# Fixed orders of instructions up to the end of a kernel with LSH attention and two expert layers

## The chip, the core and the metric

The kernel runs on one core of a Trainium2 chip. The metric is the time of one execution on the device in microseconds. Five instruction streams run side by side on the core: TensorE (PE in the profile, its weight loads PEld), VectorE (DVE), ScalarE (ACT), GpSimd (POOL) and SyncE (SP), which here only issues DMAs. Each stream runs in the order in which its instructions were written, and waits for others by semaphores.

## What is computed

The attention works on 2 x 8 heads with 768 positions of width 64. A query sees only the keys of its own hash bucket. The result, 1536 tokens of width 512, goes through two layers without any norm or residual:

```python
x = np.ascontiguousarray(attn_out.transpose(0, 2, 1, 3)).reshape(B * S, H * D)
h = x @ w_in            # 512 -> 2048
x = (h - np.tanh(h)) @ w_out
g = x @ w_gate          # 512 -> 1536
val = x @ w_val
out = (g / (1 + np.exp(-g)) * val) @ w_out2
```

## The kernel before

All work is declared as operations: each call of `op` in the kernel notes the engines that may do it with an assumed time for each, what it reads and writes, and a due time. An operation is one instruction or a short run of them, and in what follows it is named by its number in the order of declaration, 0 to 3380. Operations 0 to 1342 are the attention, 1343 to 3380 the two layers. `Plan.order` (line 182) then plays the operations through once while the program is built, and the sequence that comes out is written into the five instruction streams. Nothing of it is decided at run time.

`ORDER` (line 66) holds a written list of operations for each engine. As long as an engine's list lasts, the engine takes its next listed operation and no other. After that it takes, among the operations that are ready by the assumed times, the one with the earliest due time, and one that two engines may do goes to the one that is free:

```python
                if at[e] < len(ORDER[e]):
                    n = ORDER[e][at[e]]
                    if n not in can or e in ops[n][8] and port > now + 1e-9:
                        continue
                    at[e] += 1
                else:
                    q = ready.get(e, [])
```

In the kernel before, the lists reach a little beyond the attention: 365 of TensorE's 817 operations, 418 of VectorE's, 350 of ScalarE's, 221 of GpSimd's and 164 of SyncE's 240.

The layers work on two halves of the tokens. A product of an input layer (`products`, line 923) multiplies a 256 x 256 block of weights by a block of the tokens with seven products instead of eight (sums of blocks are formed first, on the weights by `sub`, lines 405 and 407, on the tokens by lines 461 to 468). Each is a group of six matmuls, since every factor is split in a high and a low part (line 955). Its result goes from PSUM to SBUF (ScalarE, lines 884, 891 and 935), is added to another's (VectorE, line 938), goes through tanh or the gate (lines 872 and 877), and is the factor of an output group (`out_group`, line 987, line 1009), again six matmuls: 384 columns wide in the first layer, 512 in the second. Output groups are copied to a staging buffer (line 1038) and added up by an accumulating DMA on GpSimd's queue: line 1046 into SBUF in the first layer, line 1055 into the output in DRAM in the second. Only the last output groups are added by VectorE (lines 1022 and 1033) and stored on SyncE's queue (line 1034).

The weights come as int64 bit patterns of doubles. `convert` (line 358) loads a chunk of 512 KB on SyncE's queue (line 371) into one of two buffers `raw`, and three VectorE instructions make f32 of it (lines 373, 376 and 379). A load waits until the conversion before the last has freed its buffer. The planner assumes 3.5 us to its landing. Splitting in high and low is a copy on ScalarE (lines 385 and 422) and a subtraction on GpSimd or VectorE (lines 387 and 424).

The operations that the prediction names: the additions 1648 and 2360 (line 872) and 2449, 2724, 2935 and 3101 (line 938), which products at the waits read; the loads 2835, 3001, 3073, 3149 and 3315 (line 371) and the first conversion step of three of them, 3002, 3150 and 3316 (line 373); conversion step 2508 (line 376); the accumulating writes 2704, 2810, 2870, 2899, 3036 and 3065 (line 1055); and 2915 (line 405), 3013 (line 387) and 3058 (line 872) ahead of them. A place is the position in TensorE's sequence, counted from 0.

Of the kernel before, what the change touches and what calls it, by code (L numbers as in the profile page):

```python
# [46 lines left out]
def chunk_keys():  # L47
# [5 lines left out]
    for i in range(NP2):  # L53
# [29 lines left out]
    """,  # L83
    DVE="""
# [18 lines left out]
    """,  # L103
    ACT="""
# [15 lines left out]
    """,  # L120
    POOL="""
# [9 lines left out]
    """,  # L131
    SP="""
# [7 lines left out]
    """,  # L140
).items()}

# [1056 lines left out]
```

## Time and profile before

| | |
|---|---|
| time, median of 3 runs | 777.51 us (776.3 to 778.58) |
| the profiled execution | 777.4 us |
| its span, first to last instruction | 775.6 us |
| PE busy | 755.5 us, 97% of the span, 4332 matmuls |
| DVE, ACT, POOL busy | 606.0, 475.6, 332.9 us |
| granted TensorE clock | 1.0 of 2.4 GHz |
| first operation of the layers to start on PE | 233 us |
| start of the product at place 353 | 256.6 us |

A row of a timeline has the start in us from the begin of the span, the length, engine and line of the source, the operation, what it writes and reads by the program's names, shapes, and how many instructions in a row it merges; in square brackets stands the idle time of the engine before it and what ended it. The ends of matmuls are modelled, so that the shown end of a group lies beyond the start of the next.

### The profile page before, as it was taken

The numbers are of one execution on the slowest core, as the hardware profiler recorded it, in microseconds if no ns is written. First come the engines' busy times: TensorE is split into PE (matmuls) and PEld (weight loads), VectorE is DVE, ScalarE is ACT, GpSimd is POOL, SyncE is SP. The second block draws the span as 40 slices with busy tenths as digits, with TensorE's granted clock in tenths as the row PEclk, the third lists the DMA queues.
The fourth block names the chain that finished last, engine by engine and source line by source line (L and its number), as shares of the span: only waits on it lengthen the run. The fifth ranks groups of instructions, "written<-read, shape, count | busy, mean of one in ns | idle before, by whom it ended". The sixth has DMA issues, their size and how long they took to land.

```text
span 775.6 us, 12370 instructions
## 1 busy us (share of the span) xinstructions
PE 755.5 (97%) x4332; PEld 663.4 (86%) x4332; DVE 606.0 (78%) x1092; ACT 475.6 (61%) x975; POOL 332.9 (43%) x357
## 2 busy tenths in 40 slices
PE   5899999999999999999999999999999999999998
PEld 2667676767668999999999999989998998989996
DVE  4988788868897967888778699898887867777355
ACT  3887778888776755565566556655554554555430
POOL 2755676767965712323333224543333332322120
PEclk9999999999999999999999999999999999999999
DMA  5573655356232052878676762333536756754685
GB/s 150 133 194 87 169 153 131 99 129 167 71 135 82 28 136 59 199 180 198 146 183 164 159 154 65 89 106 123 190 85 168 165 110 139 163 110 67 123 169 197
DMA packets 38717, 104.23 MB, mean 134 GB/s; under 512 B 4704, under 2 KB 10080, under 8 KB 38656
## 3 DMA queue, kind: packets, MB, share of 16 engines
q1 hardware_dynamic: 28288, 71.06, 29.7%
q0 software_dynamic: 9904, 31.59, 23.7%
q10 hardware_dynamic: 464, 0.80, 0.5%
q8 instruction: 34, 0.56, 0.3%
q14 instruction: 27, 0.22, 0.1%
HBM read 49.17 MB, written 18.87 MB: 88 GB/s over the span
## 4 chain that ended last, share of the span: by engine, by line
PE 88%; DVE 5%; DMA 3%; ACT 1%; issue 1%; POOL 1%; SPq 0%; ACTq 0%; DVEq 0%; POOLq 0%
PE bs L955 30%; PE t L1009 15%; PE s L746 8%; PE t L776 8%; PE x L799 8%; PE h L1009 8%; PE x L1009 5%; DMA raw<-in_w 2%; PE x L955 2%; PE t L955 2%; DVE m L756 1%; PE h L955 1%; DMA raw<-in_kT 1%; DVE ct L872 1%; PE h L709 1%
## 5 line engine op out<-in xcount | busy, mean ns | idle before, releaser
L955 PE MATMUL bs<-x,wi 128*128 128x384 f32 x1200 | 233.4, 336 | 3.6 <-DVE ct L938 3.6
L955 PEld LDWEIGHTS bs<-x,wi 128*128 128x128 f32 x1200 | 210.4, 188 | 10.8 <-DVE ct L938 5.7
L765 POOL TENSOR_SCALAR ct<-ct,r 128x768 f32<-128x768 f32 x96 | 93.5, 979 | 40.7 <-DVE r L764 28.5
L756 DVE TENSOR_REDUCE m<-s 128x1 f32<-128x768 f32 x96 | 91.1, 952 | 23.0 <-PE s L746 20.5
L746 PE MATMUL s<-op 128*128 128x384 f32 x384 | 93.9, 369 | 1.7 <-ACT ct L758 1.5
L758 ACT ACTIVATE ct<-s,m 128x768 f32<-128x768 f32 x96 | 86.7, 904 | 14.0 <-DVE m L756 7.4
L935 ACT ACTIVATE ct<-bs 128x384 f32<-128x384 f32 x120 | 58.8, 491 | 48.7 <-PE bs L955 48.2
L776 PE MATMUL t<-csb,ct 128*128 128x128 f32 x576 | 82.8, 276 | 1.5 <-DVE pt L782 0.9
L776 PEld LDWEIGHTS t<-csb,ct 128*128 128x128 f32 x576 | 66.7, 140 | 20.3 <-POOL ct L765 6.0
L746 PEld LDWEIGHTS s<-op 128*128 128x128 f32 x384 | 65.3, 193 | 16.1 <-ACT ct L758 9.8
L1009 PE MATMUL t<-op,wo 128*128 128x384 f32 x384 | 76.5, 335 | 0.0
L782 ACT ACTIVATE pt<-t 128x384 f32<-128x384 f32 x129 | 60.3, 492 | 26.2 <-PE t L776 25.9
L799 PE MATMUL x<-pt,v 128*64 128x384 f32 x384 | 69.0, 495 | 0.0
L1009 PEld LDWEIGHTS t<-op,wo 128*128 128x128 f32 x384 | 67.2, 188 | 0.8 <-DVE op L872 0.4
L1009 PE MATMUL t<-wo,op 128*128 128x512 f32 x264 | 67.8, 393 | 0.0
L387 POOL TENSOR_TENSOR wi<-fs,wi 128x512 fp32r<-128x512 f32 (+1 forms) x27 | 42.1, 1559 | 57.0 <-ACT wi L385 57.0
L872 POOL TENSOR_TENSOR ct<-ct 128x384 f32<-128x384 f32 x22 | 23.0, 1046 | 82.7 <-ACT ct L891 62.7
L1009 PEld LDWEIGHTS t<-wo,op 128*128 128x128 f32 x264 | 48.9, 188 | 7.9
L1046 POOL DMA_DIRECT2D acc<-ct x24 | 21.0, 875 | 72.3 <-ACT ct L1038 29.4
L385 ACT ACTIVATE wi<-fs 128x512 fp32r<-128x512 f32 (+1 forms) x60 | 41.8, 701 | 14.3 <-PE bs L955 4.0
L799 PEld LDWEIGHTS x<-pt,v 128*64 128x64 f32 x384 | 24.7, 136 | 28.7 <-issue 28.5
L955 PE MATMUL bs<-op,wi 128*128 128x384 f32 x240 | 47.5, 335 | 0.0
(165 smaller groups left out, 1385.0 us busy)
## 6 DMA issues: line engine op xcount, KB each, us to landing
raw<-in_w SPq DMA_DIRECT2D x68, 512.0 KB, 3.7
acc<-ct POOLq DMA_DIRECT2D x24, 768.0 KB, 6.0
out<-acc POOLq DMA_DIRECT2D x16, 768.0 KB, 7.6
op<-raw SPq DMA_DIRECT2D x42, 192.0 KB, 3.4
op<-f SPq DMA_DIRECT2D x56, 96.0 KB, 2.6
v<-in_v SPq DMA_DIRECT2D x8, 384.0 KB, 4.1
out<-acc SPq DMA_DIRECT2D x4, 768.0 KB, 3.8
acc<-out SPq DMA_DIRECT2D x4, 768.0 KB, 4.5
```

The source lines that it names most:

```text
L385: op({"ACT": act(n)}, lambda e: e.activation(out=hi, in_=src, func=ACTF.Copy), r=rk, w=[wk + (0,)], due=due, late=late)
L387: op({"POOL": pool(n), "DVE": dve(n)}, lambda e: e.tensor_tensor(out=lo, in0=src, in1=hi.bitcast(F32), op=ALU.subtract), r=rk + [wk + (0,) ...
L746: g.matmul(out=s[:, kh, 0:TB], lhsT=(b, a)[first][:, q0], rhs=ks[kh][0 if first else 1], start=first, stop=not first,)
L756: op({"DVE": 0.87}, lambda g: g.tensor_reduce(out=m, in_=sv, axis=AX.XY, op=ALU.max, negate=True), r=[sk + (0,), sk + (1,)], w=[mk])
L758: op({"ACT": 0.9}, lambda g: g.activation(out=p.rearrange("p (a b) -> p a b", a=2), in_=sv, func=ACTF.Exp, bias=m, accum_out=sm), r=[sk + ...
L765: op({"POOL": 0.91}, lambda g: g.tensor_scalar(out=p, in0=p, scalar1=r, scalar2=1.0, op0=ALU.mult, op1=ALU.mult), r=[pk, rk], w=[pk])
L776: g.transpose(out=t_t[z][:, kt * 128:(kt + 1) * 128], in_=p[:, z * TB + kt * 128:z * TB + (kt + 1) * 128], identity=ident)
L782: g.activation(out=dst, in_=src, func=ACTF.Copy) if g is nc.scalar else g.tensor_copy(dst, src),
L799: g.matmul(out=x[r, :], lhsT=v[:, kt, r], rhs=pt_t[ptks[e][1]][:, kt, :], start=(kt == 0), stop=(kt == NKT - 1), tile_position=(0, 64 * e),)
L935: op({"ACT": act(TB)}, lambda e: e.activation(out=dst, in_=bank(), func=ACTF.Copy), r=[bk], w=dk, due=due)
L955: e.matmul(out=bank(), lhsT=w[:, wpart, wi * 256 + k * 128:wi * 256 + k * 128 + 128], rhs=x_at(sb, xn, xpart, k), start=first and m == 0, ...
L1009: e.matmul(out=ps(), lhsT=lhs, rhs=rhs, start=c == 0, stop=c == 5)
```

## The change

The five written lists go on to the last operation. On TensorE the old list's first 353 entries stay, and then the order is another one up to place 748, and from 749 on as before. 65 operations that VectorE did are in GpSimd's list and 28 of GpSimd's in VectorE's, 25 of ScalarE's are in VectorE's and 13 of VectorE's in ScalarE's. All operations, their shapes, buffers and what they wait for are the same. Of the diff, the lists of GpSimd and SyncE are shown whole, of the others the rows that carry the operations named above:

```diff
--- before.py
+++ after.py
@@ -79,7 +79,29 @@
...
-        1429 1340 1423 1341 1468 1456 1484 1446 1454 1452 1450 1462 1466 1482 1464 1522 1509 1476 1474 1505 1552
+        1429 1340 1423 1341 1468 1456 1484 1446 1454 1462 1450 1482 1452 1466 1464 1522 1474 1509 1476 1489 1511
+        1505 1513 1552 1503 1519 1526 1534 1507 1540 1542 1589 1524 1532 1605 1547 1550 1573 1577 1554 1575 1587
...
+        1656 1711 1696 1704 1671 1698 1675 1694 1709 1727 1725 1707 1719 1754 1741 1737 1717 1732 1745 1743 1735
...
+        2269 2282 2275 2304 2308 2302 2314 2306 2322 2316 2349 2330 2357 2355 2351 2361 2366 2353 2325 2389 2364
+        2387 2395 2368 2401 2391 2399 2405 2407 2397 2414 2417 2412 2437 2441 2448 2439 2453 2457 2479 2473 2477
...
+        2645 2640 2633 2682 2649 2689 2684 2693 2691 2709 2663 2715 2719 2705 2723 2711 2698 2702 2713 2734 2731
...
+        2903 2905 2924 2926 2930 2932 2934 2938 2943 2946 2960 2955 2949 2962 2953 2964 2974 2951 2977 3016 3014
...
+        3090 3063 3096 3100 3104 3071 3109 3112 3115 3117 3119 3121 3126 3128 3130 3135 3140 3143 3147 3161 3180
...
+        3344 3347 3351 3355 3358 3361 3365 3368 3371 3375 3378
...
@@ -98,8 +120,39 @@
...
-        1431 1561 1387 1562 1424 1563 1660 1426 1469 1428 1457 1344 1346 1486 1455 1459 1451 1461 1463 1467 1350
-        1353 1354 1488 1477 1475 1479
+        1431 1561 1387 1562 1424 1563 1660 1426 1469 1428 1457 1463 1344 1455 1459 1451 1461 1486 1565 1467 1483
+        1354 1353 1477 1479 1566 1481 1360 1512 1490 1358 1661 1514 1520 1488 1527 1473 1516 1518 1541 1535 1531
...
+        1789 1648 1697 1672 1801 1790 1712 1791 1802 1714 1699 1803 1701 1710 1703 1805 1729 1720 1906 1806 1907
...
+        2360 2466 2327 2468 2469 2365 2369 2396 2507 2470 2390 2392 2402 2400 2406 2508 2408 2394 2409 2511 2426
+        2416 2418 2413 2422 2509 2442 2449 2443 2411 2445 2454 2458 2456 2450 2427 2452 2430 2512 2460 2429 2513
...
+        2832 2642 2692 2716 2706 2826 2644 2724 2755 2836 2833 2837 2699 2838 2834 2701 2736 2718 2728 2697 2843
...
+        3011 2896 2929 3078 3150 3079 3151 2935 3080 2939 2940 2948 2937 2956 3152 2957 2959 2965 2942 2963 2975
...
+        3160 3031 3169 3170 3033 3029 3048 3060 3175 3068 3240 3241 3062 3242 3050 3093 3177 3244 3040 3316 3095
+        3317 3245 3101 3105 3106 3246 3318 3108 3114 3179 3247 3248 3249 3122 3123 3125 3131 3132 3136 3137 3141
...
+        3379
...
@@ -115,8 +168,33 @@
...
-        1384 1430 1386 1432 1425 1342 1427 1343 1349 1470 1458 1485 1357 1447 1347 1359 1460 1453 1472 1352 1487
-        1483 1465 1523 1510 1355 1567 1478 1506
+        1384 1430 1386 1432 1425 1342 1427 1343 1349 1458 1357 1447 1470 1347 1359 1460 1472 1485 1523 1453 1487
+        1352 1510 1355 1475 1478 1465 1480 1506 1528 1515 1567 1517 1553 1504 1530 1508 1536 1569 1525 1533 1538
...
+        3334 3342 3349
...
@@ -127,7 +205,15 @@
...
-        1445 1315 1400 1333 1335 1325 1496 1404 1502 1422 1406 1433 1564 1345 1471 1351 1348 1358 1360 1356
+        1445 1315 1400 1333 1335 1325 1496 1404 1502 1422 1406 1433 1564 1345 1346 1471 1348 1351 1350 1356 1529
+        1568 1546 1570 1521 1609 1572 1594 1549 1630 1638 1686 1689 1687 1658 1691 1693 1706 1793 1808 1734 1810
+        1716 1812 1753 1761 1781 1910 1916 1829 1931 1839 1932 1857 1876 1884 1904 2033 2039 1952 1960 2054 1962
+        2058 2055 1980 1977 2056 1999 2060 2009 2027 2024 2083 2085 2075 2132 2100 2103 2151 2238 2161 2176 2179
+        2340 2341 2342 2198 2223 2226 2346 2285 2299 2266 2281 2291 2324 2379 2382 2319 2380 2297 2329 2363 2384
+        2321 2420 2386 2421 2434 2404 2472 2424 2518 2520 2493 2590 2591 2592 2594 2539 2567 2662 2673 2674 2679
+        2612 2681 2637 2749 2753 2639 2750 2751 2695 2648 2757 2726 2839 2828 2840 2708 2841 2771 2779 2915 2704
+        2916 2802 2917 2733 2861 2923 2921 2810 2870 3006 2892 2945 3013 2899 2966 3081 3082 3083 2980 3154 2976
+        2968 3087 3171 3172 3173 3058 3036 3111 3065 3103 3142 3251 3202 3326 3224 3231 3269 3277 3298 3303 3343
...
@@ -136,7 +222,11 @@
...
-        1182 1179 1207 1394 1434 1211 1440 1216 1491 1497 1556 1560 1659 1665
+        1182 1179 1207 1394 1434 1211 1440 1216 1491 1497 1556 1560 1659 1665 1677 1782 1681 1788 1800 1804 1905
+        1911 1923 2028 1927 2046 2034 2110 2050 2122 2116 2227 2126 2233 2332 2336 2370 2374 2461 2467 2506 2510
+        2582 2586 2651 2657 2489 2536 2665 2669 2741 2745 2817 2574 2823 2831 2835 2620 2911 2907 2983 2989 2997
+        3001 3073 3077 3149 3155 3163 3167 3239 3243 3315 3321 3328 3352 3362 3330 3338 3372 3346 3354 3357 3360
+        3364 3367 3370 3374 3377 3380
...
```

## Rows read from the trace of the kernel before

**Rows 1.** Chain that ended last: shares on the page, and from 680 us, start, us, what:

```profile
PE 88%; DVE 5%; DMA 3%; ACT 1%; issue 1%; POOL 1%; SPq 0%; ACTq 0%; DVEq 0%; POOLq 0%
...
694.82 1.39 PE t L1009 x6
696.21 3.12 PE bs L955 x18
```

**Rows 2.** TensorE's timeline at the end: start, us, engine line op out<-in xcount:

```profile
768.82 1.52 PE L1009 MATMUL x<-wo,op 128*128 128x512 f32 x6
770.18 1.52 PE L1009 MATMUL h<-wo,op 128*128 128x512 f32 x6
```

**Rows 3.** Windows: stretch, length, busy us of PE, PEld, DVE, ACT, POOL (x), PEclk, DMA, GB/s:

```profile
256.00:776.00 520.00, 511.43 (x2789) 488.82 (x2787) 398.80 (x687) 277.87 (x550) 166.59 (x138) 1.00 0.57 136
500.00:530.00 30.00, 28.27 (x153) 26.59 (x152) 28.52 (x47) 17.20 (x32) 12.33 (x9) 1.00 0.28 90
```

**Rows 4.** TensorE's timeline at its six waits from 256 us on:

```profile
315.78 1.34 PE L1009 MATMUL h<-op,wo 128*128 128x384 f32 x6 [0.30 <-DVE op L872]
...
490.36 1.32 PE L1009 MATMUL h<-op,wo 128*128 128x384 f32 x6 [0.37 <-DVE ct L872]
...
509.02 1.34 PE L955 MATMUL bs<-x,wi 128*128 128x384 f32 x6 [1.73 <-DVE ct L938]
...
586.87 2.37 PE L955 MATMUL bs<-x,wi 128*128 128x384 f32 x12 [0.48 <-DVE ct L938]
...
645.64 1.68 PE L955 MATMUL bs<-x,wi 128*128 128x384 f32 x8 [0.66 <-DVE ct L938]
...
692.47 2.35 PE L955 MATMUL bs<-x,wi 128*128 128x384 f32 x12 [0.71 <-DVE ct L938]
```

**Rows 5.** Waits of TensorE from 256 us on: us in total, times, longest:

```profile
PE bs L955 <- DVE ct L938: 3.6, 4, 1.7
```

**Rows 6.** VectorE's timeline before 692 us:

```profile
690.32 0.43 DVE L373 TENSOR_SCALAR f<-raw 128x512 uint32<-128x512 uint32 x1 [2.33 <-DMA raw<-in_w]
...
691.87 0.55 DVE L938 TENSOR_TENSOR ct<-bs,ct 128x384 f32<-128x384 f32 x1
```

**Rows 7.** Waits of VectorE for weight chunks, from 256 us on:

```profile
DVE fs L373 <- DMA raw<-in_w: 5.8, 4, 3.6
...
DVE f L373 <- DMA raw<-in_w: 5.2, 3, 2.3
```

**Rows 8.** Landing of the loads of line 371 issued at 683.8 us, and at 646.2 us:

```profile
DMA to landing us min/median/max: 6.5/6.5/6.5
...
DMA to landing us min/median/max: 3.4/3.4/3.4
```

**Rows 9.** GpSimd's timeline from 680 us:

```profile
681.36 1.30 POOL L1055 DMA_DIRECT2D out<-acc  x1 [1.23 <-ACT acc L1038]
```

**Rows 10.** DMA issues on the page: issue, xcount, KB each, median us to landing:

```profile
acc<-ct POOLq DMA_DIRECT2D x24, 768.0 KB, 6.0
out<-acc POOLq DMA_DIRECT2D x16, 768.0 KB, 7.6
```

**Rows 11.** VectorE's timeline, three long instructions:

```profile
311.83 2.04 DVE L407 TENSOR_TENSOR fs<-fs 128x256 f32<-128x256 f32 x1
...
502.73 1.79 DVE L373 TENSOR_SCALAR fs<-raw 128x512 uint32<-128x512 uint32 x1
504.44 2.05 DVE L468 TENSOR_TENSOR acc<-acc 128x768 f32<-128x768 f32 x1
```

**Rows 12.** GpSimd's timeline from 310 us:

```profile
311.74 1.84 POOL L387 TENSOR_TENSOR wi<-fs,wi 128x768 fp32r<-128x768 f32 x1
```

**Rows 13.** Source line 407: ns min/median/max, first and last start:

```profile
L407 DVE TENSOR_TENSOR fs<-fs x25: 408/425/2036, 227.2 to 697.5; 128x256 f32<-128x256 f32 x25
```

**Rows 14.** Source line 872, additions on the two engines:

```profile
L872 DVE TENSOR_TENSOR ct<-bs,ct x52: 541/550/558, 248.2 to 759.5; 128x384 f32<-128x384 f32 x52
...
L872 POOL TENSOR_TENSOR ct<-ct x22: 1003/1014/1712, 255.3 to 737.4; 128x384 f32<-128x384 f32 x22
```

61 rows, old and new, of tables (ACT, DVE, PE) are left out of this document.

## The prediction

> **What bounds the kernel now.** I read the page first. The chain that ended last lies on TensorE for 88% of the span, and only small shares are left for the other engines [rows 1]. A busy TensorE is not by itself a TensorE at its peak, so the next view is where nothing disturbs it. In the chain three products of the expert layers (six matmuls of 384 columns each) take 3.12 us, 1.04 us for one, and a group of the second output layer (six of 512 columns) takes 1.39 us [rows 1]; at the end of the program such groups start 1.36 us apart [rows 2]. The shown end of a group lies 0.16 us behind the start of the next (1.52 against 1.36), which has to be added to every idle time of TensorE.
>
> From there the ideal of the stretch that the change can touch can be counted. The new lists differ from what ran before from place 353 of TensorE's list on (places count from 0, operations by their number in order of declaration), which is the product that starts at 256.6 us. From 256 us on there are 2789 matmuls [rows 3]; 72 groups of six are of the 512-column kind, 432 matmuls (six pairs of chunks, two halves of the tokens, six groups each). 2357 x 1.04/6 + 432 x 1.36/6 = 408.5 + 97.9 = 506.4 us, or 508.6 us with 1.39. The stretch runs from 256.0 to the end of the last group, 770.18 + 1.52 = 771.7 us [rows 2], so 515.7 us. **About 7.1 us are lost on TensorE**, and that is nearly all that an order can win here: behind the last product there is one addition and one write, and the lists end in the same order as before.
>
> Where the 7.1 us lie is told by the timeline of TensorE in this stretch: six waits, at 316, 490, 509, 587, 646 and 692 us, all of them for VectorE (DVE below), with 0.30, 0.37, 1.73, 0.48, 0.66 and 0.71 us of idle time [rows 4]. With 0.16 us each they cost 0.46, 0.53, 1.89, 0.64, 0.82 and 0.87 us, in all 5.2 us. Four of the six, 3.6 us of idle time, are for the addition at line 938 [rows 5]. Behind each wait the array also needs a little longer: twelve matmuls from 692.47 on took 2.35 us where 2 x 1.04 + 0.16 = 2.24 are due [rows 4], 0.11 us, and six of these are 0.7 us. That makes 5.9 us; 1.2 us are spread over smaller delays.
>
> **Why DVE is late there** has two causes, and the change has to be weighed against both.
>
> The first is a transfer. The product at 692.47 waits for the addition of operation 3101. On DVE that addition stands behind the first steps of two weight conversions, and the second of these (3316, line 373) had DVE idle for 2.33 us until its weight chunk had landed [rows 6]. In this stretch DVE waits 11.0 us for such landings, 7 times [rows 7]. This load took 6.5 us from issue to landing, another one 3.4 us [rows 8]. The slow one was issued at 683.8, 2.4 us after GpSimd had issued an accumulating write of 768 KB at 681.4, whose landing takes 7.6 us in the median [rows 9, 10]; the fast one had none of these in flight just before. The stalls of TensorE at 587, 646 and 692 us are all of this kind, 2.3 us.
>
> The second cause is crowding on DVE, and instructions of DVE that stand still beside one of GpSimd (locks, below). From 500 to 530 us DVE is busy for 28.5 of 30 us [rows 3]. At 311.83 a block subtraction (line 407) takes 2.04 us where its median is 0.42, beside a GpSimd subtraction that began at 311.74; at 502.73 and 504.44 two DVE instructions take 1.79 and 2.05 us [rows 11 to 13]. The largest stall of TensorE follows at once, the 1.89 us at 509 us. With those at 316 and 490 us the second kind has 2.9 us.
>
> **The change, part by part.** No operation is added or taken away; the lists only fix the order of operations 1343 to 3380 and the engine of those that two engines may do. Nothing is decided at run time, so a longer list costs nothing itself.
>
> Engines. 65 operations go from DVE to GpSimd and 28 come back, 25 go from ScalarE to DVE and 13 back. An addition of 128x384 takes 0.55 us on DVE and 1.01 us on GpSimd [rows 14], so GpSimd gets some 37 x 1.0 = 37 us more on its 166.6 us, 22%, and DVE some 37 x 0.55 - 12 x 0.55 = 14 us less on its 398.8 us [rows 3]. GpSimd's extra time lies beside TensorE: in the new list no product that takes a GpSimd result comes closer than two products behind the sum of GpSimd's work for it. That cover is gone where an addition of GpSimd is followed by a write or a lock.
>
> The loads. The weight loads on SP's queue keep their engine and nearly their order; each still waits for the conversion that frees its buffer. What moves are the accumulating writes on GpSimd's queue. Before, write 2704 can be issued once TensorE has done place 649; now it stands behind 2915, a subtraction that went to GpSimd and whose queue needs place 674. Write 2899 goes from place 699 to 711 (behind 3013), 3036 from 729 to 742 (behind 3058), 3065 from 739 to 749. The three loads that came late, 2835, 3149 and 3315, stay at places 651, 700 and 739. So none of them has a fresh write ahead of it any more; their landing should fall from 6.5 to about 3.4 us [rows 8]. At 690 us DVE would then wait 2.33 - 3.1 < 0, not at all. The additions behind them are late no longer, and next in turn is nothing nearer than the two conversions themselves. This is worth 0.64 + 0.82 + 0.87 + 3 x 0.11 = **2.7 us**. What is late instead are the writes; their staging buffers are taken again 12 products later at the soonest, 12.5 us against 7.6. In the first layer two writes get only 6 products (6.2 us) where 9 were usual, and their landing takes 6.0 us in the median [rows 10]: up to half a microsecond of waiting for the engine that fills the buffer again, with the product that needs it five places off, so nothing on TensorE.
>
> The crowding. Before place 592 (509 us) the old list has 14 DVE operations after the product at place 583, and DVE ran from 500 to 509 us without a pause; the new one has 14 operations for products from place 581 on, two products (2.1 us) more room, and conversion step 2508 stands earlier. The operations ahead of places 409 and 576 are pulled apart in the same way (1648 is now needed at place 413 and not 409). All three gone is worth 0.46 + 0.53 + 1.89 + 3 x 0.11 = **3.2 us**. Of the 1.2 us of small delays I take 0.5 as gone, since those behind 587 us follow the stalls there.
>
> New stalls. What the trace of before doesn't show is where the new order is locked. Upwards: today's two stalls that began with a lock cost 0.46 + 1.89 + 2 x 0.11 = 2.6 us; 22% more GpSimd work and more products that lie within five places of the last product they depend on (128 before, 214 now) make 2.6 x 1.22 x 1.67 = 5.3 us. Downwards: 0, if no lock falls on such a place; below that nothing, since the 7.1 us are counted already. I take 2.6 us, the measured one, since the places are tighter but DVE has 14 us more air.
>
> A rule speaks against the move to GpSimd. The Trainium skill (Perfetto Trace Analysis, Optimizing Scalar/DVE Operations) says that shifting work between GpSimd and DVE might not help, since the two share a read port; SBUF — State Buffer, Who interferes with whom, says that the one that comes second blocks for the whole instruction. The rows at 311.7 to 313.9 us agree: 2.04 for 0.42 us. By that rule the 3.2 us of crowding stay, which is the first rival below.
>
> **Sum.** -2.7 - 3.2 - 0.5 + 2.6 = -3.8 us. The profiled execution took 777.4 us, 0.1 below the median of 777.5; 777.4 - 3.8 = **773.6 us**.
>
> **Rivals.** (1) *Crowding stays.* What DVE gives away comes back as locks: only the 2.7 us of the transfers are won, and 22% more on the 2.6 us of locks, 0.6, is lost: 777.4 - 2.1 = 775.3 us. For it are the two long instructions at 503 to 506 us; against it is that DVE's instructions at 509 us get two products more room whatever GpSimd does. (2) *The writes meet other loads.* A write issued later is still 768 KB. If loads 3001 or 3073, now next to writes 2810 and 2870, block DVE as 3149 did, the 2.7 us stay: 776.3 us. Against it: behind 3002 the next operation needed is due eight products later, more than the 6.5 us of a landing. (3) *Locks on tight places, slower.* Three long locks reached TensorE so far (311.8, 502.7, 504.4 us). With 1.22 x 1.67 as many, 6.1, each at the longest here, 2.04 - 0.42 = 1.62 us, and 0.11 for the restart, 10.6 us are lost, and with the 0.7 us of small delays 11.3 against 7.1 today: 777.4 + 4.2 = 781.6 us. It decides for slower (by over 2.3 us) from 1.43 us per lock. Against it: most products have work of others behind them, and a lock of 2.04 us at 311.8 cost TensorE just 0.46. (4) *The lists say what the planner chose anyway.* That can be seen to be false: 131 operations change engine, and TensorE's own order changes at place 353.
>
> **Chances.** The forecast has 0.64, rival 1 0.16, rival 2 0.08, rival 3 0.12, rival 4 next to nothing. A measurement of this kernel can tell about 0.3%, 2.3 us, from no change. The forecast lies 3.8 us below; with new stalls at their upper end of 5.3 us it would be only 1.1 below, so a small part of it, 0.03, counts as no change. Faster 0.61, within 0.3% 0.27, slower 0.12. The range: downwards all 7.1 us are gone at 770.3 us; upwards it reaches past rivals 1 and 2 to 777.8 us, and leaves out rival 3 and the last of the others.
>
> **What would show it.** Right: TensorE's wait for line 938 falls from 3.6 us to under 1 us, DVE's wait for the weight chunks from 11.0 to under 5 us, loads issued near 577, 637 and 684 us land within 4 us, GpSimd's busy time grows by 30 to 40 us and DVE's falls by 10 to 20. Wrong: loads that land after 6 us with DVE idle and an addition of line 938 behind; DVE instructions of 1.5 to 2.5 us followed by a wait of TensorE; or waits of TensorE for ScalarE, which it has none of in this stretch now.

## The result and the profile after

The changed kernel takes 785.55 us in the median of four executions (784.21 to 788.54), the kernel before 777.33 us beside it: a ratio of 1.011, with a 95% interval of 1.0076 to 1.0144. It is slower by about 8 us where 3.8 us of gain were forecast. The profiled execution is the longest of the four, 788.54 us, 11.1 above the 777.4 us of the profiled execution before, so terms that are read from this trace are set against 788.54. The other three executions are 2.3 to 4.3 us shorter; no trace shows which of the stalls below is smaller there.

In the changed kernel all lines behind the lists stand 90 lower: the products at line 1045 (955 before), the output groups at 1099 (1009), the additions at 1028 and 962 (938, 872), the accumulating writes at 1136 and 1145 (1046, 1055), the loads at 461 (371). In the kernels of the experiments these line numbers are smaller by some 8 (line 1045 is 1037 or 1036 there, 962 is 954 or 953).

The windows of the changed kernel (the columns of [rows 3]), the whole stretch first, then three pieces behind long waits:

```profile
256.00:787.00 531.00, 514.70 (x2790) 492.17 (x2788) 387.29 (x662) 260.19 (x540) 207.69 (x175) 0.99 0.56 133
493.00:500.00 7.00, 6.10 (x26) 6.10 (x27) 3.50 (x7) 2.69 (x7) 3.42 (x3) 0.76 0.28 56
643.00:648.00 5.00, 4.19 (x15) 4.19 (x16) 3.34 (x7) 0.45 (x1) 0.00 (x0) 0.66 0.68 134
714.00:720.00 6.00, 5.47 (x29) 5.21 (x30) 5.86 (x11) 4.06 (x8) 1.83 (x2) 1.00 0.57 101
```

GpSimd is busy for 207.7 us against 166.6 in [rows 3], VectorE for 387.3 against 398.8: the work went where the lists say. The waits of TensorE from 256 us on (to [rows 5]; us in total, times, longest):

```profile
PE bs L1045 <- DVE ct L1028: 4.0, 2, 3.6
PE h L1099 <- DVE ct L962: 4.0, 1, 4.0
PE bs L1045 <- DVE ct L962: 1.9, 1, 1.9
PE t L1099 <- DVE op L962: 1.1, 1, 1.1
PE bs L1045 <- DVE op L553: 0.9, 1, 0.9
PE t L1099 <- DVE ct L1128: 0.3, 1, 0.3
```

None of the six waits of [rows 4] is left, but these are new, and three of them are long (3.95, 1.91 and 3.58 us). TensorE's timeline at those three, with the products behind them (to [rows 4]):

```profile
493.90 1.99 PE L1099 MATMUL h<-op,wo 128*128 128x384 f32 x6 [3.95 <-DVE ct L962]
495.69 2.12 PE L1099 MATMUL t<-op,wo 128*128 128x384 f32 x6
497.61 1.26 PE L1045 MATMUL bs<-x,wi 128*128 128x384 f32 x6
...
643.81 4.96 PE L1045 MATMUL bs<-x,wi 128*128 128x384 f32 x18 [1.91 <-DVE ct L962]
...
714.52 2.35 PE L1045 MATMUL bs<-x,wi 128*128 128x384 f32 x12 [3.58 <-DVE ct L1028]
```

Set out as TensorE's time above its undisturbed pitch (1.04 us for a group of 384 columns, 1.39 for one of 512), start by start from place 340 on, the kernel before has 8.0 us and the changed one 19.1. The difference of 11.1 us is that of the spans (786.8 and 775.6). Of the 19.1 us, 5.75 belong to the stall at 494 us (4.12 for the wait, 1.63 for the two slow products behind it, 1.79 and 1.92 us where 1.04 are due), 3.76 to that at 644 us (2.07 and 1.69), 3.85 to that at 715 us; then 1.35 at 477 us, 1.17 at 262 us, 0.64 at 727 us and 0.61 at 439 us. The three long stalls make 13.4 us.

**At 494 us** a staging buffer is asked for before its last write has landed. GpSimd's, ScalarE's and VectorE's timelines:

```profile
481.23 0.88 POOL L1136 DMA_DIRECT2D acc<-ct  x1 [2.87 <-ACT ct L1128]
```
```profile
490.63 1.28 ACT L981 ACT_TABLE_LOAD   x1 [3.62 <-DMA acc<-ct]
491.92 0.49 ACT L981 ACTIVATE ct<-h 128x384 f32<-128x384 f32 x1
492.31 0.48 ACT L967 ACTIVATE op<-bs 128x384 fp32r<-128x384 f32 x1
```
```profile
492.83 0.56 DVE L962 TENSOR_TENSOR op<-bs,op 128x384 fp32r<-128x384 f32 x1 [4.96 <-ACT op L967]
493.30 0.55 DVE L962 TENSOR_TENSOR ct<-h,ct 128x384 f32<-128x384 f32 x1
```

Write 2324 is issued at 481.23 and lands at 490.56, 9.3 us later (7.3 us in the kernel before; why it took longer here was not tried). Operation 2359 (line 981) stands first on ScalarE's queue and needs its buffer: ScalarE stands still for 3.62 us and then loads a table for 1.28 us. Operation 2312 behind it was ready since 486.6 us; VectorE waits 4.96 us for it, and TensorE for VectorE. The 0.61 us at 439 us are a small case of the same: there a copy on VectorE waits 1.21 us for such a landing.

**At 644 and 715 us** a write is held until the one before it has landed. GpSimd's timeline, and VectorE's behind it, first for 644 us:

```profile
638.62 1.28 POOL L1145 DMA_DIRECT2D out<-acc  x1 [7.44 <-ACT wi L475]
639.44 1.24 POOL L497 TENSOR_TENSOR fs<-fs 128x256 f32<-128x256 f32 x1
```
```profile
640.71 0.43 DVE L497 TENSOR_TENSOR fs<-fs 128x256 f32<-128x256 f32 x1 [3.26 <-POOL fs L497]
...
643.22 1.01 DVE L962 TENSOR_TENSOR ct<-bs,ct 128x384 f32<-128x384 f32 x2
```

The input of write 2870 was there at 632.48, but write 2810 ahead of it lands only at 638.30, and 2870 starts at 638.62. The subtraction behind it on GpSimd is late by that, VectorE stands 3.26 us for it, and the addition for TensorE's product comes at 643.22. The same for 715 us:

```profile
694.77 1.31 POOL L1145 DMA_DIRECT2D out<-acc  x1
702.34 1.28 POOL L1145 DMA_DIRECT2D out<-acc  x1 [6.26 <-ACT ct L1025]
710.20 1.28 POOL L1145 DMA_DIRECT2D out<-acc  x1 [6.59 <-issue]
711.02 1.49 POOL L962 TENSOR_TENSOR ct<-ct 128x384 f32<-128x384 f32 x1
```
```profile
713.45 0.56 DVE L962 TENSOR_TENSOR op<-bs,op 128x384 fp32r<-128x384 f32 x1 [7.13 <-ACT op L967]
713.92 0.55 DVE L1028 TENSOR_TENSOR ct<-bs,ct 128x384 f32<-128x384 f32 x1
```

Writes 3036, 3111 and 3065 stand one behind the other. 3036 lands at 702.01 and 3111 starts at 702.34; 3111 lands at 709.88 and 3065 starts at 710.20, though its input was there at 695.3. In front of it GpSimd waits 6.59 us for nothing that the profile shows. The multiplication 3103 behind it (711.02) is late by that, then two copies on ScalarE, then VectorE's addition for TensorE. By its declaration a write waits only for the last write to the same rows, four writes back. Yet all eight held writes of this execution start 0.32 to 0.37 us after the one ahead has landed. In the kernel before they are issued 9 to 13 us apart and land after 7.2 to 10.1 us, each before the next one is issued, so no row of that trace shows a hold.

### The profile page after: what moved, and what is told of

Its sections match the earlier page's. It is cut to its first block, busy times and chain, and to the rows that moved or that the text cites. A ratio compares the mean times of both kernels' runs of the same rounds, so it can differ in the third digit from the quotient of the medians.

```text
span 786.8 us, 12350 instructions
## 1 busy us (share of the span) xinstructions
PE 758.1 (96%) x4332; PEld 665.9 (85%) x4332; DVE 593.1 (75%) x1067; ACT 457.6 (58%) x963; POOL 374.3 (48%) x394
## 5 line engine op out<-in xcount | busy, mean ns | idle before, releaser
L477 POOL TENSOR_TENSOR wi<-fs,wi 128x512 fp32r<-128x512 f32 (+1 forms) x29 | 47.9, 1656 | 35.1 <-ACT wi L475 22.0
L962 POOL TENSOR_TENSOR ct<-ct 128x384 f32<-128x384 f32 x24 | 28.0, 1167 | 58.3 <-ACT ct L981 42.3
L1145 POOL DMA_DIRECT2D out<-acc x16 | 20.7, 1296 | 67.2 <-PE bs L1045 20.7
L962 POOL TENSOR_TENSOR op<-ct,op 128x384 fp32r<-128x384 f32 x28 | 31.5, 1130 | 35.9 <-ACT op L967 35.8
```

What stands on the lines that cost most here:

```text
L477: op({"POOL": pool(n), "DVE": dve(n)}, lambda e: e.tensor_tensor(out=lo, in0=src, in1=hi.bitcast(F32), op=ALU.subtract), r=rk + [wk + (0,) ...
L962: op({"DVE": dve(TB), "POOL": pool(TB)} if port else {"DVE": dve(TB) + 0.01}, lambda e: e.tensor_tensor(out=now(dst), in0=now(a), in1=b, o ...
```

## The experiments

The **theory**: the changed lists bring two waits that were priced at nothing, for a staging buffer on ScalarE's queue and for the write ahead on GpSimd's. The **rivals**: the greater share of GpSimd as such (locks, crowding); a stall early that only shifts what follows; and a gain from the loads that never came.

**Half of the lists each.** The lists of one kernel up to place 600 of TensorE's list, of the other behind it.

```diff
-ORDER: the changed lists
+ORDER: changed lists to place 600, then the order before (first_part)
+ORDER: the order before to place 600, then the changed lists (second_part)
```

> The changed lists up to place 600 of TensorE's list (about 520 us), behind it the order and the engines of the kernel before. Places the loss. In the two traces TensorE's time above its undisturbed pitch from place 340 to 600 is 10.8 us in the changed kernel and 4.8 in the one before, and behind place 600 it is 8.3 against 3.3. If each half loses by a wait of its own (a staging buffer asked for too early at 494 us, writes held on GpSimd's queue at 644 and 715 us), this kernel loses the 6.0 us of the first half and nothing behind: 783.5 us. If the loss came from the greater share of GpSimd's work as such (locks), it would go with the number of operations moved to GpSimd, and the stalls of the first half would come back at other places. If a stall of the first half only put off a delay that comes anyway, 777 to 778 us.

> The order and the engines of the kernel before up to place 600, behind it the changed lists. If the held writes of the second half are a loss of their own, they are here too, with the stalls near 638 and 708 us (the changed kernel's, some 6 us earlier), and the second half costs 8.3 us instead of 3.3: 777.4 + 5.0 = 782.4 us. If these two stalls came only because the first half was late, 775 to 778 us.

Measured: the first half alone 783.84 us (783.36 to 784.41), a ratio of 1.0077 [1.0056, 1.0098]; the second half alone 781.91 us (779.75 to 784.63), 1.0054 [1.0037, 1.007]. Each half loses by itself. In the first the stall at 494 us is there (TensorE waits 3.0 us for the addition that is line 962 in the changed kernel), in the second the one near 704 us (3.27 us and 2.80 of slower products behind it); the one at 644 us is not there, so it stands on an edge. That both times come so near to the forecasts is in part luck. In the profiled execution of the first half TensorE loses 4.5 us more than before up to place 600, where 6.0 were forecast, and 2.5 us lie ahead of place 340, where the changed kernel, with the same lists there, loses 0.2. In that of the second half 2.9 us are lost more than before behind place 600, where 5.0 were forecast.

**The writes where their input is ready.**

```diff
 GpSimd:
-2915 2704 2916 2802 2917 2733 2861 2923 2921 2810 2870 3006
+2704 2839 2828 2840 2708 2841 2733 2771 2779 2915 2916 2802 2810 2917 2861 2923 2921 2870 3006
...
-2892 2945 3013 2899 2966
+2892 2899 2945 3013 2966
...
-2976 2968 3087 3171 3172 3173 3058 3036 3111 3065 3103
+2968 3036 3087 3171 3172 3173 3058 3065 3111 3103
```

> All of the changed lists but one thing: eleven accumulating writes of the second layer stand on GpSimd's queue where their input is ready, and not behind later additions and subtractions. Engines, and the order on the four other queues, stay as changed. Theory of the held writes: the stalls at 643.8 us (2.07 us and 1.69 us of slower products behind it) and at 714.5 us (3.85 us) go, 7.6 us: 785.5 - 7.6 = 777.9 us; the stall at 494 us stays. Rival, locks and crowding by GpSimd's 41 us of added work: this work is all still there, so 784.5 to 786.5 us.

Measured: 783.8 us (783.28 to 786.79), 1.0088 [1.0066, 1.011]; the profiled execution took 783.99, 4.6 below that of the changed kernel. The expected 777.9 was set against the median, though the stalls were those of the profiled execution, so 780.9 was due. The stalls at 644 and 715 us are gone as the theory says, and a new one of 3.12 us stands at 653 us. VectorE's timeline there, and the landing of the load that it waits for:

```profile
651.12 0.43 DVE L455 TENSOR_SCALAR f<-raw 128x512 uint32<-128x512 uint32 x1 [3.58 <-DMA raw<-in_w]
...
652.67 0.55 DVE L1020 TENSOR_TENSOR ct<-bs,ct 128x384 f32<-128x384 f32 x1
```
```profile
DMA to landing us min/median/max: 7.0/7.0/7.0
```

This is load 3149, issued at 644.1, 1.8 us after write 2899 (642.28). It is the very wait of the kernel before [rows 6, 8], come back with the write: the prediction's first mechanism, seen from the other side. A write held late costs one wait, a write put early the other.

**The staging buffer.**

```diff
 TensorE:
-2325 2389 2364 2387 2395 2368 2401
+2325 2364 2387 2395 2368 2389 2401
 ScalarE:
-2383 2359 2312 2362 2465 2326 2328 2388
+2383 2312 2362 2465 2326 2328 2359 2388
 VectorE:
-2313 2360 2466 2327 2468 2469 2365
+2313 2466 2327 2468 2469 2360 2365
```

> All of the changed lists but three operations: the output group 2389 on TensorE four products later, and the filling of its staging buffer (2359 on ScalarE) and the addition 2360 on VectorE later by as much. Theory of the staging buffer: ScalarE no longer stands at 2359 waiting for write 2324 to land while TensorE needs what is behind it; the stall of 4.12 us at 494 us goes and with it the 1.63 us of slower products behind: 785.5 - 5.75 = 779.8 us. If the slower products come from something else than the long wait (the clock falls there anyway), only 4.1 us go: 781.4 us. If crowding on VectorE is what makes the product late, the wait turns up there instead: 784 to 786 us.

Measured: 782.42 us (781.01 to 785.89), 1.0062 [1.0039, 1.0084]; the profiled execution took 782.23, 6.3 below that of the changed kernel. The stall at 494 us is down to 0.40 us and the slow products behind it are gone with it. Here too the stall at 644 us is nearly gone (0.65 us), and the one at 706 us is as long as before, 3.35 us, with 2.84 us of slower products behind it, which the changed kernel's own trace did not have. The forecast of 5.75 us off, which from 788.54 is 782.8, is met in the sum by luck, since these two differences nearly cancel; what shows the cause is the stall at 494 us itself. The window at 706 us, columns as above:

```profile
706.00:713.00 7.00, 6.92 (x22) 6.45 (x23) 6.86 (x9) 3.15 (x7) 3.17 (x2) 0.57 0.65 96
```

**The engines.**

```diff
-the engine of each operation as changed
+DVE/POOL as in the kernel before, at the place where the changed order starts it
```

> All of the changed order, but every operation that went from VectorE to GpSimd or back runs on the engine that it had before, at the place where the changed order starts it. Theory of locks and crowding by GpSimd's added 41 us: the loss goes with it, 777 to 780 us. Theory of the written places (writes behind one another, a staging buffer asked for early): the writes stand as close together, and VectorE has its 13 us back; the stall at 262 us (1.2 us, a lock) goes, those at 494 and 715 us stay: 783 to 787 us.

Measured: 795.24 us (790.37 to 796.6), 1.0209 [1.0168, 1.025], slower than either forecast. The windows of this run, and three of TensorE's waits:

```profile
256.00:793.00 537.00, 518.16 (x2789) 494.23 (x2787) 409.97 (x699) 261.11 (x540) 168.96 (x138) 0.99 0.56 132
```
```profile
PE bs L1037 <- DVE ct L954: 3.8, 2, 3.2
PE h L1091 <- DVE ct L954: 3.2, 1, 3.2
PE bs L1037 <- DVE ct L1020: 3.1, 1, 3.1
```

The three long stalls are all there (3.36, 3.39 and 3.24 us above the pitch at 497, 649 and 719 us), without GpSimd's added work, and others come on top (1.87 us at 338, 1.44 us at 489). So the rival of GpSimd's share falls: in this order the move to GpSimd is worth 795.24 - 785.55 = 9.7 us. The order was written for the moved operations, so this does not say what the move is worth in another order. The Trainium skill (Perfetto Trace Analysis, Optimizing Scalar/DVE Operations) warns that work shifted between GpSimd and VectorE might bring nothing since they share a read port; in this order the measurement differs, and it decides.

**One write, and three, moved in the kernel before.**

```diff
 GpSimd (one_write):
-2976 3087 3160 3027 3036 3089 3172 3058 3065 3103
+2976 3087 3160 3027 3089 3172 3058 3036 3065 3103
 GpSimd (three_writes):
-2726 2733 ... 2892 2899 2937 2945 ... 3058 3065 3103 3111
+2726 2704 2733 ... 2892 2937 2899 2945 ... 3058 3103 3065 3111
```

> The kernel before with its lists written out in full and one thing moved: write 3036 stands directly in front of write 3065 on GpSimd's queue, 11 us later than before. Theory of the held writes: 3036 starts near 681 us and lands 7.5 us later, and 3065 starts only then, near 689 us, though its input is there at 681; GpSimd stands for some 6.5 us. What stands behind, the multiplication 3103 first, is that much late; the stall of TensorE behind it at about 705 us is up to 3 us: 777 to 780.5 us. If writes to different rows can be in flight together, 3065 starts within 1.5 us of 3036 and the time is that of before, 776.5 to 778 us.

Measured: 777.27 us (776.1 to 781.25), 0.9997 [0.998, 1.0014]: no difference. GpSimd's timeline shows the hold with nothing else changed:

```profile
684.28 1.28 POOL L1136 DMA_DIRECT2D out<-acc  x1
691.76 1.29 POOL L1136 DMA_DIRECT2D out<-acc  x1 [6.20 <-ACT ct L1016]
```

3036 starts at 684.28 and lands at 691.44; 3065, ready at 685.2, starts at 691.76. The hold is as the theory says, but the stall of up to 3 us near 705 us that was forecast from it did not come: the multiplication 3103 behind it had its input only at 695.5. The stall of the kernel before at 692 us is gone. The profiled execution is the longest of the ten (781.25 us); what it has more, 4.3 us of TensorE, stands at 334 us, long before the write that was moved.

> The kernel before with its lists written out in full and one part of the change alone: writes 2704, 2899 and 3065 each behind the next addition on GpSimd's queue (2726, 2937, 3103), so that loads 2835, 3149 and 3315 have no fresh write ahead of them. By the transfer term of the prediction these three land after 3 to 5 us in place of 6.4 to 6.5, and the stalls at 587, 646 and 692 us with 0.11 us each behind them go: 777.4 - 2.7 = 774.7 us. If holding the next write (each now starts when the one moved has landed, some 6 to 7 us later than before) makes new stalls, 777 to 780 us.

Measured: 787.53 us (784.83 to 789.39), 1.011 [1.0082, 1.0137], as large a loss as that of the whole change, from three moved writes. The three loads land after 4.0, 3.4 and 3.3 us, and the stalls at 587, 646 and 692 us are gone, just as the transfer term had it. But a stall of 6.60 us with 2.25 us of slower products stands at 604 us. GpSimd's, VectorE's and TensorE's timelines:

```profile
586.33 1.32 POOL L1136 DMA_DIRECT2D out<-acc  x1
595.88 1.31 POOL L1136 DMA_DIRECT2D out<-acc  x1 [8.23 <-issue]
596.72 1.25 POOL L488 TENSOR_TENSOR fs<-fs 128x256 f32<-128x256 f32 x1
```
```profile
598.00 0.43 DVE L488 TENSOR_TENSOR fs<-fs 128x256 f32<-128x256 f32 x1 [8.13 <-POOL fs L488]
```
```profile
604.46 4.21 PE L1036 MATMUL bs<-x,wi 128*128 128x384 f32 x12 [6.43 <-DVE ct L1019]
```

Write 2733 is held behind 2704 for 8.23 us; subtraction 2840 behind it on GpSimd starts at 596.72 where it started at 590.2 before, and VectorE stands for it at its own next subtraction. The delay runs on along the queue: 2899 starts at 652.56 and takes 10.3 us, 2945 behind it is held for 9.29 us, 2976 for 4.29 and 3036 for 1.81. The second stall, 3.52 us at 682 us, is both mechanisms at once: VectorE waits 3.31 us there for a load issued 3.2 us after the held write 2976, which took 5.7 us.

**What holds a write: the pieces.**

```diff
-o = out[sb * S + t * TB:sb * S + t * TB + TB, :].rearrange("(j p) c -> p j c", p=128)
+o = out[sb * S + t * TB:sb * S + t * TB + TB, :].rearrange("(p j) c -> p j c", j=3)
...
-lhs, rhs = gs[f][gpart][:, m * 128:m * 128 + 128], w[:, wpart, :]
+lhs, rhs = gs[f][gpart].rearrange("p (a b) -> p a b", b=3)[:, :, m], w[:, wpart, :]
```

> All of the changed lists; the second output layer gives every partition three neighbouring rows of the output in place of rows 128 apart, so that an accumulating write of 768 KB has pieces of 6 KB, as those of the first layer have, in place of 2 KB (the weights of its matmuls are read with a stride of three). Nothing in the program makes a write wait for the one before it to other rows. If a write is held for the number of pieces of the one in flight, the holds of up to 6.6 us are gone and with them the stalls at 644 and 715 us: 785.5 - 7.6 = 777.9 us in the profiled run. If it is held because it goes to DRAM, or for its size, the holds stay: 784 to 788 us. If the strided weights cost TensorE time, its groups of the second output layer start more than 1.39 us apart.

Measured: 782.72 us in the median (one execution of eight took 1989 us, for which no profile stands), 1.006 [1.0038, 1.0082]; the profiled execution took 781.7, 6.8 below that of the changed kernel, where 7.6 were expected. TensorE's waits of 0.9 us and more from 256 us on are three, the first of them that at 494 us:

```profile
PE h L1091 <- DVE ct L954: 2.8, 1, 2.8
PE t L1091 <- DVE op L954: 1.1, 1, 1.1
PE bs L1037 <- DVE op L545: 0.9, 1, 0.9
```

GpSimd's timeline, and the rows of the weight loads of both kernels (ns min/median/max):

```profile
691.11 0.87 POOL L1137 DMA_DIRECT2D out<-acc  x1
696.94 1.77 POOL L1137 DMA_DIRECT2D out<-acc  x2 [4.96 <-ACT ct L973]
```
```profile
L1091 PEld LDWEIGHTS t<-wo,op x264: 250/252/253, 514.7 to 772.6; 128*128 128x128 f32 x132
```
```profile
L1099 PEld LDWEIGHTS t<-wo,op x264: 187/188/188, 516.2 to 779.6; 128*128 128x128 f32 x132
```

Writes 3111 and 3065 start one right behind the other (696.94 and, in the same row, 697.49), before the one ahead has landed, and no write of the second layer starts more than 0.65 us after its input and the queue are ready. The stalls at 644 and 715 us are gone; that at 494 us is left. So what holds a write is how the writes are cut in pieces, and not their 768 KB or their target. Whether it is the number of the pieces or their size, and whether those of the write in flight or of the one that waits, is not told apart, since all writes changed together. The Trainium skill (DMA: Bandwidth & Descriptors, SWDGE vs HWDGE vs iDMA) says that GpSimd appends the descriptors of its DMAs to rings in a reserved part of SBUF; a ring that holds one such write and not two would fit, but no run here shows the ring itself. The kernel sets `dynamic_dma_scratch_size=1024` (line 1279 of the changed kernel); a run with a larger value would be the test, and there is none. The strided weights cost 252 ns a load where 188 stood, and an output group 1.407 us where 1.387 stood (means of some 70 groups), 0.02 x 72 = 1.4 us. Counted start by start behind place 600, the products between these groups lie 0.8 to 1.0 us further above their pitch too, in each kernel with strided weights against the same lists without them, so some 2.3 us in all.

> The kernel before with its lists written out in full and with neighbouring rows for each partition in the second output layer (pieces of 6 KB in its writes). Here no write was held, so nothing is to be won on that side. If a load comes late behind a write because of that write's many pieces, loads 2835, 3149 and 3315 land sooner than 6.4 us and the three stalls of 2.7 us go: 774.7 us. If it is the bytes that they share the DMA engines with, the landings stay above 6 us: 776.5 to 778 us.

Measured: 777.83 us (776.4 to 779.02), 0.999 [0.9973, 1.0006]. The three loads land after 5.7, 5.4 and 5.4 us, between the two forecasts, and the stalls at 587, 646 and 692 us are gone; that gain of 2.7 us is nearly what the strided weights cost. Why the loads are still slower than 4 us was not tried.

**Mended versions.**

```diff
+the order before up to place 375 (mended) or 363 (mended2), then the changed lists
+TensorE, ScalarE, VectorE: 2389, 2359 and 2360 later, as above
+ScalarE: 2271 2290   (was 2290 2271)
+VectorE: 2274 2287   (was 2287 2274)
+GpSimd: 2976 2968 3036 3087 3171 3172 3173 3058 3065 3111 3103
+VectorE, mended2 alone: 2197 ahead of 2344, 2240 ahead of 2248
```

> The changed lists with four mends: the order of the kernel before up to place 375 (the stall of 1.2 us at 262 us, a long instruction of VectorE beside one of GpSimd); a copy on ScalarE and the addition 2287 each put behind one that a product waits for (1.3 us at 477 us); group 2389 four products later (494 us); and of the writes only 3036, 3065 and 3111 where their input is ready (715 us), the five before them left where the change put them, since the run with all of them early had a load come late behind 2899. The run with 2389 later had 13.1 us of TensorE above its undisturbed pitch, 6.2 of them at 706 us: 13.1 - 6.2 - 1.3 - 1.0 = 4.6 us against 8.0 in the kernel before, so 777.4 - 3.4 = 774.0 us, faster than both. If waits only change place with every mend (a load late behind 3036 or 3065, as behind 2899), 777 to 780 us.

> As the mended lists, but the order of the kernel before ends at place 363, where both lists have the same products behind them, in place of 375 (in the mended run a product at 283 us waited for VectorE, 0.85 us), and VectorE copies the result for write 2198 ahead of a weight subtraction and adds 2240 ahead of 2248 (0.90 us at 464 us). The mended run had 5.2 us of TensorE above its undisturbed pitch; 1.9 less makes 3.3 against 8.0 in the kernel before: 777.4 - 4.7 = 772.7 us for an execution without new waits. The mended kernel's median lay 2.4 us above its profiled execution, and if that is so here too, 775 us.

> The lists of the run mended2 and neighbouring rows for each partition in the second output layer, so that no write is held. If the spread of the mended kernel between executions comes from writes held for one another, its median falls to its best executions: 772 to 773.5 us. If the holds no longer cost anything in these lists, as that of mended2.

Measured: mended 776.14 us (773.73 to 778.11), 0.997 [0.9953, 0.9987], so that the 774.0 expected was met by its profiled execution (773.73) and not by its median; mended2 774.55 us (771.97 to 777.23), **0.9948 [0.9924, 0.9973]**, half a per cent faster than the kernel before and faster than the changed one; its profiled execution took 772.57, against 772.7 expected. It keeps the added work of GpSimd (210.2 us busy from 256 us on), so that work as such is not what the changed kernel loses by. Its waits of TensorE from 256 us on are these two, and 3.7 us are left above the pitch, where the kernel before has 8.0:

```profile
PE bs L1037 <- DVE ct L954: 0.3, 1, 0.3
PE t L1091 <- DVE ct L1120: 0.3, 1, 0.3
```

With the rows side by side it takes 775.11 us (774.19 to 775.71), 0.996 [0.9945, 0.9976]. Its median is not better and its best is 2.2 us longer, about what the strided weights cost, but eleven executions lie within 1.5 us where the eight of mended2 spread over 5.3. That holds are the source of the spread is not shown: the kernel before, in whose trace no write is held, spreads over 6.9 us in 24 executions, and with the rows side by side over 2.6 us in ten.

## Why the prediction was wrong

**What bounds the kernel, the 7.1 us.** Right. An order can win what TensorE waits: all six waits of [rows 4] are gone from the changed kernel, and mended2 wins 3 us in the median.

**The transfers, -2.7 us.** Right in mechanism and size. Loads 2835, 3149 and 3315 land after 3.9, 4.4 and 3.1 us (6.4, 6.4 and 6.5 before), the three stalls are gone, VectorE's wait for chunks fell from 11.0 us [rows 7] to 4.7, and with write 2899 put back ahead of load 3149 in early_writes the wait came back.

**The crowding, -3.2 us.** The three stalls are gone, but one of the same kind came at 477 us (1.35 us). The **engines** term was right: 41.1 us more on GpSimd (37 estimated), 11.5 less on VectorE (14), and engines_back shows that the move helps in this order.

**New stalls, +2.6 us of locks.** About right for what it covers: two locks reached TensorE, at 262 us (1.17 us, VectorE's 2.58 us beside a GpSimd operation of 1.84) and at 727 us (0.64 us, VectorE's 3.01 us from 718.77 on beside a GpSimd subtraction of 2.36, and no pause of VectorE until then). With the 1.35 us of crowding that makes 3.2 us.

**The step that failed** is the sentence "What is late instead are the writes; their staging buffers are taken again 12 products later at the soonest, 12.5 us against 7.6", with the one behind it on the first layer, "so nothing on TensorE". The first asked only who takes the buffer of a late write. It did not ask what is queued behind the write on GpSimd, nor whether a write behind another has to wait for its landing. The first stood in reach, as the new list has 3036, 3111 and 3065 in a row and 3103 behind them; for the second the trace of before has no row. It was priced at 0 and took 3.76 + 3.85 = 7.6 us in the profiled execution: the writes were held until the one ahead had landed, and what GpSimd had behind them came late. The second took the median landing of 6.0 us [rows 10] for a margin of 6 products and the cover of five places for enough. The landing took 9.3 us (the longest of this kind before took 8.4), ScalarE's queue stood behind it with what the next products needed, and 5.75 us were lost.

By the prediction's own sum: -2.7 - 3.2 - 0.5 + 2.6 = -3.8 us, and with the 13.4 us of these two it is +9.6, against the 11.1 measured between the two profiled executions; the 1.5 us between the two were not taken apart. The medians lie only 8.2 us apart; which stalls are smaller in the other executions no trace shows.

**The rivals.** Rival 1 (crowding stays) falls: the three stalls of crowding are gone, and the loss grows when GpSimd's added work is taken back (engines_back). Rival 2 (writes meet other loads): loads 3001 and 3073 landed after 5.0 and 4.1 us and stalled nothing. Rival 3 had the sign and not the cause: two locks of 1.8 us together, not six of 10.6. Rival 4 is excluded by the moved work.

**The marks named beforehand.** VectorE's wait for chunks (4.7 us) and its busy time came out as named for right, and two of the three landings; load 3149 took 4.4 us where 4 were named, and GpSimd's busy time grew by 41.1 where 30 to 40 were. TensorE's wait for line 938 did not fall: 4.0 us (line 1028 now), no longer for a load but behind a held write. Of the marks for wrong one came, the long instructions of VectorE (2.58 and 3.01 us) with a wait of TensorE behind them, and it is the smaller part of the loss.

## What to carry to other kernels

When a write is moved on an engine's queue, ask three things: what is queued behind it, whether the write ahead has landed by then (here it mattered for writes in pieces of 2 KB, not of 6 KB), and who takes its buffer next on an in-order engine. Count with the longest landing in the trace, not the median. The same write put early can make a weight load late, so the place to look for is the one behind the load and a full landing away from the write ahead.

## What the runs showed of the hardware

- A second accumulating write of 768 KB in pieces of 2 KB starts 0.32 to 0.37 us after the one in flight has landed, and GpSimd stands for up to 9.29 us with it (in three_writes); in pieces of 6 KB two start one right behind the other.
- What a long wait costs TensorE beyond itself varies. Behind 3.95 us of idle time the granted clock was 0.76 over 493 to 500 us, behind 1.91 us it was 0.66 over 643 to 648 us, and single groups took 1.79 and 1.92 us for 1.04, near the lower of the two levels (1.2 for 2.4 GHz). Behind 3.58 us at 714 us it stayed at 1.00, while in late_489 it was 0.57 over 706 to 713 us behind 3.19 us at the same product.
- A weight load of 128x128 read with a stride of three takes 252 ns in place of 188, and the groups of 512 columns hide all but 0.02 us of six such loads; the products between them lose 0.8 to 1.0 us in all.
- At 490.63 us ScalarE loaded a table for 1.28 us only after its wait of 3.62 us for a buffer had ended, so it came on top of that wait.
